# Moving the fifth product of the experts' second stage ahead of the reads of its PSUM bank, with two preparations moved

## The chip, the cores and the metric

One core of one Trainium2 chip. The time is device microseconds of one execution of the program. TensorE (PE) multiplies, VectorE (DVE), ScalarE (ACT) and GpSimd (POOL) prepare operands and read results, SyncE (SP) issues most of the transfers.

## What is computed

Linear attention with random features, then a dense mixture of four experts over its output `x` (2304 rows of 512):

```
p = domain_probs / (domain_probs.sum(-1, keepdims=True) + 1e-09)
out = np.zeros((N, D), dtype=np.float32)
for e in range(E):
    h = np.maximum(x @ w1[e], 0.0)
    out += p[:, e:e + 1] * (h @ w2[e])
```

With N = 2304, D = 512, E = 4 and 1024 hidden columns. The attention part is not touched by the change.

## The kernel before

**Visits.** The hidden columns of the four experts are cut into 8 halves of 512. One visit multiplies one half with a block of rows of `x`: its first stage is `h = relu(x @ w1)`, its second adds `p * (h @ w2)` to the accumulators `acc`. The first 11 visits are done by `plain`, the 16 that follow (row blocks of 7 tiles of 128 rows, twice 8 halves) by `fast`. Of the last 8 visits seven are "deep" (`DEEP`): in the trace they run from about 620 to 908 us. The last visit of all is not deep.

**Exact products from halves.** Each operand is split (`split`, L490 to L495) into a high part by ACT (a copy, L492) and a low part (L495, a subtraction, on POOL here), and each product is three matmuls: high by high, high by low, low by high.

**Seven products in place of eight.** `fast` computes the first stage of a visit as seven block products in each of two groups (`p1` to `p7`), whose sums are formed by ACT and DVE. A deep visit does the second stage (`sevens`, L909) in the same way: for three pairs of row tiles (`QS3`) it forms sums of `h` (`t1` in the tile `va`, `t2` in `vb`, `r11`) and uses sums of `w2` (`B`, tiles `w2s`). The operands made from sums of `h` are the pairs `T[5]`, `T[6]`, `T[7]` (tile `t_hl`). Tile 3 of the seven is computed directly (`outputs`). The second stage runs in this order on PE:

1. `X[q][:, L]`: a direct product, into the left half of the PSUM bank of `X[q]`, q = 0 to 2, amid `p7(1)`, `p3(1)` and `p4(1)` of the first stage;
2. the **fifth product**, into the right half of the same three banks, from `T[5]` (18 matmuls, L907, tiles `w2s` and `t_hl`);
3. the block product `Z` (18 matmuls), then tile 3 (12 matmuls of 512 columns, L676 to L678);
4. the sixth product, added to the left halves of `X[q]`; then a product `block(1, 1)` added to the right halves; then the seventh, and a last product from the four parts of `hs` that were overwritten.

Before the sixth product is added to the left half of `X[q]`, DVE adds what stands there to `acc` (`gather`, L693): "the reads" below. Dependencies are kept by whole PSUM tile: `X[q]` is one tile of one bank, so in this kernel an instruction that writes its right half waits for an earlier one in the program that reads its left half.

**Order of work.** Every engine does its instructions in the order in which the program issues them (`manual_schedule`); a wait holds up all that is queued behind it. Two generators, advanced by `next(...)` at fixed places, prepare the coming visit: `sides(v + 1)` the operands of the first stage (tiles `w1ah`, `w1al` from `w1r` by `direct`, split by ACT and POOL; tiles `w1sh`, `w1sl` by `fetched`, two transfers from DRAM, issued from POOL's queue), and `w2_sides(v + 1)` (`start_sides2`, `on_sides2`) those of the second (`sums_of`, four POOL additions L540 to L543 into `w2f`, then splits). After `fetched` the order in a deep visit is: `T[5]` split, then the first `sums_of` of the next visit, then all of `sevens`.

Of the kernel before, what the change touches and what calls it, by code (L numbers as in the profile page):

```python
# [9 lines left out]
ALU = mybir.AluOpType  # L10
# [4 lines left out]
def attention_moe(ctx, tc, kT, qT, kd, qd, kn, qn, vn, omT, probs, w1, w2, out):  # L15
# [10 lines left out]
    nc = tc.nc  # L26
# [42 lines left out]
    def f32(ap):  # L69
        return ap.bitcast(F32)  # L70
# [42 lines left out]
    class Pair:  # L113
# [7 lines left out]
        def load(self, which, eng=nc.sync):  # L121
            src = {"k": kT, "q": qT}[which[0]][self.b, self.hp][:, TILES[int(which[1])]]
            t = xop([P, src.shape[1]], which, F32)
            setattr(self, which, t)
            eng.dma_start(t[:D], src)
# [364 lines left out]
    def split(t, a, c, hi, lo):  # L490
        if hi is nc.scalar:
            hi.activation(a, t, AF.Copy)  # L492
        else:
            hi.tensor_copy(a, t)
        lo.tensor_tensor(c, t, f32(a), ALU.subtract)  # L495
# [95 lines left out]
    def sides(v):  # L591

        tiles = [raw.pop((v, "w1", i)) for i in range(2)]
        A, S = {}, {}

        def direct(i):
            A[i] = ah, al = pair_of(("w1ah", 3 * H), ("w1al", 3 * H))
            for r, cs in ((tiles[i][:, :2 * H], slice(0, 2 * H)), (tiles[i][:, 3 * H:], slice(2 * H, 3 * H))):
                split(r, ah[:, cs], al[:, cs], nc.scalar, nc.gpsimd)

        def add(i):
            r11, r12, r21, r22 = (tiles[i][:, j * H:(j + 1) * H] for j in range(4))
            nc.vector.tensor_tensor(r22, r21, r22, ALU.add)
            nc.vector.tensor_tensor(r21, r11, r21, ALU.subtract)
            nc.vector.tensor_tensor(r11, r22, r11, ALU.subtract)
            nc.vector.tensor_tensor(r12, r12, r11, ALU.subtract)

        def summed(i):
            S[i] = sh, sl = pair_of(("w1sh", 4 * H), ("w1sl", 4 * H))
            split(tiles[i], sh, sl, nc.scalar, nc.gpsimd)  # L610
            made[v, i] = S[i]
            parts(i)
            load("w1")

        def parts(i):
            W[v, "w1", i] = {
                p: tuple(x[:, j * H:(j + 1) * H] for x in t)
                for t, at in ((A[i], (1, 2, 4)), (S[i], (6, 3, 7, 5)))
                for j, p in enumerate(at)
            }  # L620

        def fetched(i):
            S[i] = pair_of(("w1sh", 4 * H), ("w1sl", 4 * H))
            for t, k in zip(S[i], kept[visits[v][1:3], i]):
                nc.gpsimd.dma_start(t, k)

        direct(0)
        if visits[v][0] < 2:
            yield
        else:  # L630
            load("w1")
            fetched(0)
            parts(0)
            fetched(1)
            yield
            direct(1)
            load("w1")
            parts(1)
            yield
            return  # L640
        direct(1)
        yield
        add(0)
        yield
        summed(0)
        yield
        add(1)
        yield
        summed(1)
        yield  # L650
# [31 lines left out]
    def gather(v, ps, t, cs=slice(0, DM)):  # L682
        _, e, _, c0, n = visits[v]
        i = c0 // P + t
        sc = pr[:, i, e:e + 1]
        if i not in acc:
            acc[i] = held([P, DM], "acc", F32)
        fresh = [h for h in (0, H) if cs.start <= h < cs.stop and (i, h) not in begun_at]
        begun_at.update((i, h) for h in fresh)
        if fresh:  # L690
            nc.scalar.activation(acc[i][:, cs], ps, AF.Copy, scale=sc)  # L691
        else:
            nc.vector.scalar_tensor_tensor(acc[i][:, cs], ps, sc, acc[i][:, cs], ALU.mult, ALU.add)  # L693
# [102 lines left out]
    def fast(v):  # L796
# [29 lines left out]
        def less(to, t, x, op=ALU.subtract):  # L826
            nc.vector.scalar_tensor_tensor(to, t, 0.0, x, ALU.max, op)  # L827

        def first_rows(t):
            return t[:, :WT]  # L830
# [71 lines left out]
        def seventh(q, to, a, b, start=True):  # L902
            for f in range(2):
                (xa, xc), (wa, wc) = a[f], b[f]
                xa, xc = (x[:, q * P:(q + 1) * P] for x in (xa, xc))
                for k, (x, w) in enumerate(((xa, wa), (xa, wc), (xc, wa))):
                    nc.tensor.matmul(to, x, w, start=(start and f + k == 0), stop=(f + k == 3), skip_group_check=not start)  # L907

        def sevens():  # L909

            L, R, QS3 = slice(0, H), slice(H, DM), range(3)

            def block(g, j):
                return [tuple(x[:, j * FH * P:j * FH * P + WT] for x in hs[2 * g + f]) for f in range(2)]

            def sums_of(i):
                return [tuple(x[:, f] for x in T[i]) for f in range(2)]

            def weights(g, cs):
                return [tuple(x[:, cs] for x in W[v, "w2", 2 * g + f]) for f in range(2)]  # L920

            def mixed(i, cs):
                return [tuple(x[:, cs] for x in B[f, i]) for f in range(2)]

            X, Z = [], []
            for q in QS3[:2]:
                X.append(bank("g2"))
                seventh(q, X[q][:, L], block(0, 0), weights(0, L))
            p7(1)
            less(t2[:, 1], last_rows(P_[1]["p5"]), t1[:, 1])  # L930
            X.append(bank("g2"))
            seventh(2, X[2][:, L], block(0, 0), weights(0, L))
            p3(1)
            less(t2[:, 0], last_rows(P_[1]["u2"]), t1[:, 0])
            p4(1)
            nc.gpsimd.tensor_tensor(r11, t2, r11, ALU.subtract)
            nc.scalar.activation(T[6][0], t2, AF.Copy)
            less(t1[:, 1], first_rows(P_[1]["u"]), t2[:, 1])
            for q in QS3:
                gather(v, X[q][:, L], q, L)  # L940
            nc.vector.tensor_tensor(T[6][1], t2, f32(T[6][0]), ALU.subtract)
            less(t1[:, 0], first_rows(P_[1]["p1"]), t2[:, 0])
            next(ready, None)
            split(r11, *T[7], nc.scalar, nc.gpsimd)
            for f in range(2):
                split(t1[:, f], *(x[:, FH * P:] for x in hs[f]), nc.scalar, nc.gpsimd)
            yield 1
            for q in QS3:
                seventh(q, X[q][:, R], sums_of(5), mixed(1, R), start=False)
            yield 1  # L950
            zs = []
            for q in QS3:
                if q < 2:
                    Z.append(bank("g2"))
                zs.append(Z[q // 2][:, q % 2 * H:(q % 2 + 1) * H])
                seventh(q, zs[q], block(1, 0), weights(1, L))
            for q in QS3:
                gather(v, zs[q], q, L)
            next(ready, None)
            yield 1  # L960
            ps = bank("g2")
            outputs(v, hs, ps, 3, range(FH))
            gather(v, ps, 3)
            on_sides2(v + 1)
            on_sides2(v + 1)
            yield 1
            for q in QS3:
                seventh(q, X[q][:, L], sums_of(6), mixed(0, L), start=False)
                gather(v, X[q], 4 + q)
            yield 1  # L970
            for q in QS3:
                seventh(q, X[q][:, R], block(1, 1), mixed(1, L), start=False)
                gather(v, X[q][:, R], 4 + q, L)
            on_sides2(v + 1)
            yield 1
            for q in QS3:
                seventh(q, X[q][:, L], sums_of(7), mixed(0, R), start=False)
                gather(v, X[q][:, L], 4 + q, R)
            on_sides2(v + 1)
            yield 1  # L980
            for q in QS3:
                seventh(q, X[q][:, L], [tuple(x[:, FH * P:] for x in hs[f]) for f in range(2)], weights(1, R), start=False)
                gather(v, X[q][:, L], q, R)
            for t in range(tiles):
                gathered(v, t)
            yield 1
# [24 lines left out]
        p5(1)  # L1011
        if deep:
            prepare()
        p3(0)
        p4(0)
        if deep:
            nc.scalar.activation(r11[:, 1], first_rows(P_[0]["u"]), AF.Relu)
            less(t1[:, 1], last_rows(P_[0]["p5"]), r11[:, 1])
            p6(1)
            split(t1, *T[5], nc.scalar, nc.gpsimd)  # L1020
            if v + 1 in DEEP:
                start_sides2(v + 1)
            yield from sevens()
            return
        prepare()
# [309 lines left out]
```

## Time and profile before

| | |
|---|---|
| median of 3 runs | 948.84 us (948.64 to 952.38) |
| the profiled execution | 949.2 us |
| its span in the trace | 947.4 us |
| mean granted clock of TensorE | 0.982 of full speed |
| busy, share of the span | PE 96%, DVE 61%, POOL 55%, ACT 50% |

Busy shares are averages over the whole program; the change is in seven visits of some 41 us each. In a row of the timeline the first number is the start in us from the span's start, the second the length (of all of them, where an `x18` merges 18 that follow each other), and the brackets hold the engine's idle time just before it with the instruction that ended it by the profile. A matmul's length is longer than the distance to the next, since matmuls are pipelined.

### The profile page before, as it was taken

The page shows a single profiled execution, that of the slowest core. Times are in us where ns is not written, and L with a number is a line of the kernel's source. Part 1 is how long each engine was busy: PE and PEld are TensorE (multiplying, and loading weights), DVE is VectorE, ACT ScalarE, POOL GpSimd, SP SyncE. Part 2 cuts the span into 40 slices and gives each one's busy share as a digit, 9 for nine tenths or more (in the row PEclk, how much of TensorE's full clock was granted, in tenths as well). Part 3 has the DMA queues.
Part 4 walks back from the last instruction along what each step waited for, and adds up shares of the span by engine and source line. Part 5 has one row for each costly group of instructions (what it writes and reads, how often), then busy time and mean ns, then how long its engine had stood idle before and what let it go on. Part 6 is the DMA issues. An engine that isn't in the chain of part 4 may idle for free. (4 is left out here: it accounts for less than half of the span.)

```text
span 947.4 us, 14345 instructions
## 1 busy us (share of the span) xinstructions
PE 906.0 (96%) x5286; PEld 804.1 (85%) x5286; DVE 574.4 (61%) x956; ACT 476.2 (50%) x1076; POOL 518.3 (55%) x459
## 2 busy tenths in 40 slices
PE   9999999999999999999999999998898989889898
PEld 9888888888788788888888898787897979779896
DVE  5665667776758636556765747845456565755643
ACT  6454767767645464455454453544544344353430
POOL 5655465655544533433444235668687786878630
PEclk9999999999999999999999999998998999999999
DMA  7563463553415454251434133624141432414212
GB/s 186 164 208 100 140 186 103 158 163 114 137 59 177 134 181 146 68 172 68 156 106 156 38 140 127 229 79 145 33 149 45 164 111 68 145 34 156 83 41 78
DMA packets 56583, 117.21 MB, mean 124 GB/s; under 512 B 9728, under 2 KB 18112, under 8 KB 56512
## 3 DMA queue, kind: packets, MB, share of 16 engines
q1 hardware_dynamic: 51664, 99.21, 33.0%
q0 software_dynamic: 4608, 16.78, 4.9%
q8 instruction: 42, 0.69, 0.3%
q10 hardware_dynamic: 240, 0.30, 0.1%
q14 instruction: 29, 0.24, 0.1%
HBM read 94.77 MB, written 21.50 MB: 123 GB/s over the span
## 5 line engine op out<-in xcount | busy, mean ns | idle before, releaser
L495 POOL TENSOR_TENSOR w2l<-w2r,w2h 128x512 fp32r<-128x512 f32 x93 | 122.4, 1325 | 141.3 <-ACT w2h L492 107.3
L693 DVE SCALAR_TENSOR_TENSOR acc<-g,pr,acc 128x512 f32<-128x512 f32 (+1 forms) x207 | 124.4, 618 | 89.6 <-PE g L678 57.0
L676 PE MATMUL g<-w2h,hh 128*128 128x512 f32 x368 | 147.2, 400 | 0.6 <-ACT hh L889 0.5
L678 PE MATMUL g<-w2h,hl 128*128 128x512 f32 x368 | 144.1, 392 | 0.0
L677 PE MATMUL g<-w2l,hh 128*128 128x512 f32 x368 | 143.8, 391 | 0.0
L854 DVE TENSOR_TENSOR sum<-g,sum 128x448 f32<-128x448 f32 x96 | 59.6, 621 | 97.4 <-PE g L843 96.5
L495 POOL TENSOR_TENSOR w1al<-w1r,w1ah 128x256 fp32r<-128x256 f32 (+1 forms) x77 | 87.2, 1151 | 50.1 <-ACT w1ah L492 47.1
L495 POOL TENSOR_TENSOR w1sl<-w1r,w1sh 128x512 fp32r<-128x512 f32 (+1 forms) x43 | 74.9, 1743 | 61.0 <-ACT w1sh L492 52.7
L859 ACT ACTIVATE hh<-sum 128x448 fp32r<-128x448 f32 (+1 forms) x96 | 50.9, 530 | 109.1 <-DVE sum L854 109.1
L860 DVE SCALAR_TENSOR_TENSOR hl<-sum,hh 128x448 fp32r<-128x448 f32 (+1 forms) x96 | 59.4, 618 | 73.0 <-ACT hh L859 73.0
L843 PE MATMUL g<-xbh,w1sh 128*128 128x448 f32 x256 | 94.0, 367 | 2.6 <-ACT sum L849 2.6
L843 PE MATMUL g<-xbl,w1sh 128*128 128x448 f32 x256 | 93.6, 366 | 0.0
L843 PE MATMUL g<-xbh,w1sl 128*128 128x448 f32 x256 | 93.4, 365 | 0.0
L849 ACT ACTIVATE sum<-g 128x448 f32<-128x448 f32 x96 | 51.7, 540 | 75.7 <-PE g L843 75.6
L907 PE MATMUL g<-w2s,t_hl 128*128 128x256 f32 x378 | 57.4, 314 | 28.1 <-ACT w1ah L492 24.2
L678 PEld LDWEIGHTS g<-w2h,hl 128*128 128x128 f32 x368 | 69.1, 188 | 16.1 <-DVE hl L890 0.7
L676 PEld LDWEIGHTS g<-w2h,hh 128*128 128x128 f32 x368 | 69.4, 188 | 14.6 <-ACT hh L889 0.9
L907 PEld LDWEIGHTS g<-w2s,t_hl 128*128 128x128 f32 x378 | 54.8, 219 | 31.1 <-ACT w1ah L492 26.3
L677 PEld LDWEIGHTS g<-w2l,hh 128*128 128x128 f32 x368 | 69.4, 189 | 12.2
L843 PE MATMUL g<-xbh,w1ah 128*128 128x448 f32 x192 | 70.7, 368 | 0.0
L843 PE MATMUL g<-xbh,w1al 128*128 128x448 f32 x192 | 70.2, 366 | 0.0
L843 PE MATMUL g<-xbl,w1ah 128*128 128x448 f32 x192 | 70.1, 365 | 0.0
(197 smaller groups left out, 2170.9 us busy)
## 6 DMA issues: line engine op xcount, KB each, us to landing
w1r<-in_w SPq DMA_DIRECT2D x54, 512.0 KB, 3.8
w2r<-in_w SPq DMA_DIRECT2D x108, 256.0 KB, 2.7
kept<-w1sh SPq DMA_DIRECT2D x16, 512.0 KB, 5.8
kept<-w1sl SPq DMA_DIRECT2D x16, 512.0 KB, 6.4
w1sh<-kept POOLq DMA_DIRECT2D x16, 512.0 KB, 5.9
w1sl<-kept POOLq DMA_DIRECT2D x16, 512.0 KB, 6.7
out<-acc SPq DMA_DIRECT2D x18, 256.0 KB, 2.0
va<-in_vn SPq DMA_DIRECT2D x14, 256.0 KB, 4.9
```

What stands on the lines that cost most here:

```text
L495: lo.tensor_tensor(c, t, f32(a), ALU.subtract)
L676: nc.tensor.matmul(ps, ha[:, ts_], wa, start=(c == 0), stop=False)
L677: nc.tensor.matmul(ps, ha[:, ts_], wc, start=False, stop=False)
L678: nc.tensor.matmul(ps, hc[:, ts_], wa, start=False, stop=(c == FH - 1))
L693: nc.vector.scalar_tensor_tensor(acc[i][:, cs], ps, sc, acc[i][:, cs], ALU.mult, ALU.add)
L843: nc.tensor.matmul(ps, a[:, w], x[:, k], start=(start and k + at == 0), stop=(k == 1 and at == 2), skip_group_check=not start)
L849: nc.scalar.activation(t, P_[g][where], AF.Copy)
L854: nc.vector.tensor_tensor(t, P_[g][where], t, ALU.add)
L859: nc.scalar.activation(ha, t, AF.Relu)
L860: nc.vector.scalar_tensor_tensor(hc, t, 0.0, f32(ha), ALU.max, ALU.subtract)
L907: nc.tensor.matmul(to, x, w, start=(start and f + k == 0), stop=(f + k == 3), skip_group_check=not start)
```

## The change

In deep visits: (a) the fifth product is issued before the three reads, which move behind the split of `T[7]`, the low part of `T[6]` and the last difference of `t1`; (b) the additions `sums_of` of the next visit's `w2` move from behind the split of `T[5]` to ahead of `p3(0)`; (c) the two halves of `sides` become four steps, fetch 0, direct 0, fetch 1, direct 1, at four places of the visit; the split of `T[7]` now comes ahead of both `direct` steps; (d) in the first deep visit, where accumulators are fresh, ten first writes of `acc` go from ACT to DVE. Counts of instructions per visit stay the same.

```diff
+        if visits[v][0] == 2:
+            for i in range(2):
+                fetched(i)
+                yield
+                direct(i)
+                load("w1")
+                parts(i)
+                yield
+            return
         direct(0)
-        if visits[v][0] < 2:
-            yield
-        else:
-            load("w1")
-            fetched(0)
-            parts(0)
-            fetched(1)
-            yield
-            direct(1)
-            load("w1")
-            parts(1)
-            yield
-            return
+        yield
         direct(1)
...
-        if fresh:
+        if fresh and v in DEEP:
+            nc.vector.tensor_scalar(acc[i][:, cs], ps, sc, None, ALU.mult)
+        elif fresh:
             nc.scalar.activation(acc[i][:, cs], ps, AF.Copy, scale=sc)
...
             less(t1[:, 1], first_rows(P_[1]["u"]), t2[:, 1])
+            nc.vector.tensor_tensor(T[6][1], t2, f32(T[6][0]), ALU.subtract)
+            for q in QS3:
+                seventh(q, X[q][:, R], sums_of(5), mixed(1, R), start=False)
+            split(r11, *T[7], nc.scalar, nc.gpsimd)
+            next(ready, None)
+            less(t1[:, 0], first_rows(P_[1]["p1"]), t2[:, 0])
             for q in QS3:
                 gather(v, X[q][:, L], q, L)
-            nc.vector.tensor_tensor(T[6][1], t2, f32(T[6][0]), ALU.subtract)
-            less(t1[:, 0], first_rows(P_[1]["p1"]), t2[:, 0])
             next(ready, None)
-            split(r11, *T[7], nc.scalar, nc.gpsimd)
             for f in range(2):
                 split(t1[:, f], *(x[:, FH * P:] for x in hs[f]), nc.scalar, nc.gpsimd)
-            yield 1
-            for q in QS3:
-                seventh(q, X[q][:, R], sums_of(5), mixed(1, R), start=False)
-            yield 1
+            yield 2
...
         if deep:
             prepare()
+            if v + 1 in DEEP:
+                start_sides2(v + 1)
         p3(0)
         p4(0)
...
             split(t1, *T[5], nc.scalar, nc.gpsimd)
-            if v + 1 in DEEP:
-                start_sides2(v + 1)
+            next(ready, None)
             yield from sevens()
```

PE's own order stays as it was, instruction by instruction; what it waits for differs. The fifth product of the fourth deep visit on PE before, with the engines that each row waits for (`g_7962`, `g_7969`, `g_7986` are the banks `X[0]`, `X[1]`, `X[2]`):

```order
L843 MATMUL g_7882<-xbh,w1al 128x448
L907 MATMUL g_7962<-w2s,t_hl 128x256 [waits DVE_49,Activation_49]
L907 MATMUL g_7962<-w2s,t_hl 128x256 [waits Pool_49] x2
L907 MATMUL g_7962<-w2s,t_hl 128x256 x3
L907 MATMUL g_7969<-w2s,t_hl 128x256 [waits DVE_49]
L907 MATMUL g_7969<-w2s,t_hl 128x256 x5
L907 MATMUL g_7986<-w2s,t_hl 128x256 [waits DVE_49]
```

The same place now (the three banks have the numbers 7966, 7973 and 7990):

```order
L842 MATMUL g_7882<-xbh,w1al 128x448
L906 MATMUL g_7966<-w2s,t_hl 128x256 [waits Activation_49]
L906 MATMUL g_7966<-w2s,t_hl 128x256 [waits Pool_49] x2
L906 MATMUL g_7966<-w2s,t_hl 128x256 x3
L906 MATMUL g_7973<-w2s,t_hl 128x256 x6
L906 MATMUL g_7990<-w2s,t_hl 128x256 x6
```

The three waits for DVE, one at each bank, are gone from the fifth product; those for ACT and POOL (the two halves of `T[5]`) stay. DVE at the same visit before (L693 are the reads, L941 the low part of `T[6]`, the last row the last difference of `t1`):

```order
L890 SCALAR_TENSOR_TENSOR hl<-g_7882,hh 128x448
L827 SCALAR_TENSOR_TENSOR va<-g_7882,vb 128x384
L693 SCALAR_TENSOR_TENSOR acc<-g_7962,pr,acc 128x256
L693 SCALAR_TENSOR_TENSOR acc<-g_7969,pr,acc 128x256
L693 SCALAR_TENSOR_TENSOR acc<-g_7986,pr,acc 128x256
L941 TENSOR_TENSOR t_hl<-vb,t_hl 128x768
L827 SCALAR_TENSOR_TENSOR va<-sum,vb 128x384
```

And now:

```order
L889 SCALAR_TENSOR_TENSOR hl<-g_7882,hh 128x448
L826 SCALAR_TENSOR_TENSOR va<-g_7882,vb 128x384
L938 TENSOR_TENSOR t_hl<-vb,t_hl 128x768
L826 SCALAR_TENSOR_TENSOR va<-sum,vb 128x384
L692 SCALAR_TENSOR_TENSOR acc<-g_7966,pr,acc 128x256
L692 SCALAR_TENSOR_TENSOR acc<-g_7973,pr,acc 128x256
L692 SCALAR_TENSOR_TENSOR acc<-g_7990,pr,acc 128x256
```

The reads stand behind the two operand steps. POOL at the same visit before (L540 to L543 are the sums of the next visit's `w2`, `t_hl<-va` and `t_hl<-r_7825` the low parts of `T[5]` and `T[7]`):

```order
L495 TENSOR_TENSOR w2s<-w2f,w2s 128x512 x2
L495 TENSOR_TENSOR t_hl<-va,t_hl 128x768
L540 TENSOR_TENSOR w2f<-w2r 128x256
L541 TENSOR_TENSOR w2f<-w2f,w2r 128x256
L542 TENSOR_TENSOR w2f<-w2r,w2f 128x256
L543 TENSOR_TENSOR w2f<-w2r 128x256
L936 TENSOR_TENSOR r_7825<-vb,r_7825 128x768
L495 TENSOR_TENSOR w1al<-w1r,w1ah 128x512
L495 TENSOR_TENSOR w1al<-w1r,w1ah 128x256
L625 DMA w1sh<-kept 128x1024
L625 DMA w1sl<-kept 128x1024
L625 DMA w1sh<-kept 128x1024
```

And now:

```order
L495 TENSOR_TENSOR w2s<-w2f,w2s 128x512 x2
L540 TENSOR_TENSOR w2f<-w2r 128x256
L541 TENSOR_TENSOR w2f<-w2f,w2r 128x256
L542 TENSOR_TENSOR w2f<-w2r,w2f 128x256
L543 TENSOR_TENSOR w2f<-w2r 128x256
L495 TENSOR_TENSOR t_hl<-va,t_hl 128x768
L625 DMA w1sh<-kept 128x1024
L625 DMA w1sl<-kept 128x1024
L935 TENSOR_TENSOR r_7825<-vb,r_7825 128x768
L495 TENSOR_TENSOR t_hl<-r_7825,t_hl 128x768
L495 TENSOR_TENSOR w1al<-w1r,w1ah 128x512
L495 TENSOR_TENSOR w1al<-w1r,w1ah 128x256
```

The sums stand ahead of the low part of `T[5]`, two of the four fetches ahead of `r11`, and the low part of `T[7]` ahead of the `w1al` pair.

## Rows read from the trace of the kernel before

**Rows 1.** The page's first part: busy time of each engine over the span.

```profile
PE 906.0 (96%) x5286; PEld 804.1 (85%) x5286; DVE 574.4 (61%) x956; ACT 476.2 (50%) x1076; POOL 518.3 (55%) x459
```

**Rows 2.** Waits of PE over the span: total us, times, longest us.

```profile
PE g L907 <- ACT w1ah L492: 24.2, 6, 4.2
```

**Rows 3.** Timeline of PE: `p4(1)`'s end, the fifth product, tile 3; visits 1, 4, 7.

```profile
641.58 0.37 PE L843 MATMUL g<-xbh,w1al 128*128 128x448 f32 x1
...
652.78 0.40 PE L676 MATMUL g<-w2h,hh 128*128 128x512 f32 x1
...
765.54 0.37 PE L843 MATMUL g<-xbh,w1al 128*128 128x448 f32 x1
770.14 3.51 PE L907 MATMUL g<-w2s,t_hl 128*128 128x256 f32 x18 [4.23 <-ACT w1ah L492]
...
776.01 0.40 PE L676 MATMUL g<-w2h,hh 128*128 128x512 f32 x1
...
778.76 2.31 PE L907 MATMUL g<-w2s,t_hl 128*128 128x256 f32 x18
...
785.16 0.28 PE L907 MATMUL g<-w2h,hh 128*128 128x256 f32 x1
...
888.33 0.37 PE L843 MATMUL g<-xbh,w1al 128*128 128x448 f32 x1
891.75 2.37 PE L907 MATMUL g<-w2s,t_hl 128*128 128x256 f32 x18 [3.06 <-ACT w1ah L492]
...
896.11 0.40 PE L676 MATMUL g<-w2h,hh 128*128 128x512 f32 x1
```

**Rows 4.** Stretches: length; PE, PEld, DVE, ACT, POOL busy (count); granted clock; DMA.

```profile
770.14:774.46 4.32, 4.32 (x23) 4.32 (x24) 3.45 (x4) 1.84 (x4) 4.32 (x6) 0.60 0.07 12
765.74:787.30 21.56, 17.33 (x121) 16.70 (x121) 15.20 (x26) 7.82 (x14) 19.18 (x19) 0.92 0.48 159
787.30:806.50 19.20, 19.20 (x104) 17.76 (x102) 9.01 (x15) 9.46 (x19) 11.85 (x11) 1.00 0.13 42
```

**Rows 5.** Timeline of DVE, fourth deep visit.

```profile
760.75 0.56 DVE L827 SCALAR_TENSOR_TENSOR va<-sum,r 128x384 f32<-128x384 f32 x1 [0.63 <-ACT r L1017]
...
765.24 1.09 DVE L827 SCALAR_TENSOR_TENSOR vb<-sum,va 128x384 f32<-128x384 f32 x1
...
769.52 1.26 DVE L693 SCALAR_TENSOR_TENSOR acc<-g,pr,acc 128x256 f32<-128x256 f32 x3
...
778.96 3.34 DVE L693 SCALAR_TENSOR_TENSOR acc<-g,pr,acc 128x512 f32<-128x512 f32 x5 [2.20 <-PE g L678]
```

**Rows 6.** Timeline of ACT (first row) and POOL, fourth deep visit.

```profile
761.35 0.85 ACT L492 ACTIVATE t_hl<-va 128x768 fp32r<-128x768 f32 x1 [0.26 <-DVE va L827]
...
757.51 1.30 POOL L495 TENSOR_TENSOR w2s<-w2f,w2s 128x512 fp32r<-128x512 f32 x1 [0.22 <-ACT w2s L492]
762.27 1.88 POOL L495 TENSOR_TENSOR t_hl<-va,t_hl 128x768 fp32r<-128x768 f32 x1 [3.46 <-ACT t_hl L492]
764.10 0.74 POOL L540 TENSOR_TENSOR w2f<-w2r 128x256 f32<-128x256 f32 x1
...
766.88 0.72 POOL L543 TENSOR_TENSOR w2f<-w2r 128x256 f32<-128x256 f32 x1
...
770.47 2.71 POOL L495 TENSOR_TENSOR w1al<-w1r,w1ah 128x512 fp32r<-128x512 f32 x2
...
777.09 2.00 POOL L495 TENSOR_TENSOR hl<-va,hh 128x384 fp32r<-128x384 f32 x2
```

**Rows 7.** Timeline of DVE, then POOL, last deep visit.

```profile
891.13 1.26 DVE L693 SCALAR_TENSOR_TENSOR acc<-g,pr,acc 128x256 f32<-128x256 f32 x3
892.31 1.90 DVE L941 TENSOR_TENSOR t_hl<-vb,t_hl 128x768 fp32r<-128x768 f32 x1
894.13 1.09 DVE L827 SCALAR_TENSOR_TENSOR va<-sum,vb 128x384 f32<-128x384 f32 x1
...
890.29 1.84 POOL L936 TENSOR_TENSOR r<-vb,r 128x768 f32<-128x768 f32 x1 [3.37 <-DVE vb L827]
```

## The prediction

> **What bounds the kernel now.** I read the busy shares first: PE is busy for 906.0 of 947.4 us, and no other engine for more than 61% [rows 1]. So time can come only from PE's idle 41 us, from PE's work at a low clock, or from PE work taken away, and this change takes none away. Next, PE's waits. One kind holds most of the idle time: six waits of up to 4.2 us, 24.2 us together, all ahead of L907 [rows 2]. The timeline shows the place, the fifth product of each deep visit: in the fourth, PE issues the last matmul of `p4(1)` at 765.54 and the first of the fifth product at 770.14 [rows 3].
>
> What ends that wait? The profile names a split of `w1ah` on ACT, which the fifth product does not read. The order of instructions tells more: at each of its three banks the product waits for DVE, and the reads of these banks begin at 769.52 [rows 5], 0.62 us before the product does. Its own operand was done long before: the low half of `T[5]` ended at 762.27 + 1.88 = 764.15 [rows 6]. I take the reads as what ends last. They are late because DVE has the differences and low parts of `p3(1)` and `p4(1)` to do first.
>
> The wait costs twice. In the 4.32 us after it the granted clock is 0.60 [rows 4], a mixture of the half level (1.2 GHz) and the full one (2.4 GHz). The 36 matmuls of the fifth product and of `Z` then take 776.01 - 770.14 = 5.87 us in the fourth visit. In the last deep visit, where the wait was 3.06 us, they take 896.11 - 891.75 = 4.36 us [rows 3], 0.12 us each.
>
> **The change, part by part.**
>
> *The fifth product ahead of the reads.* From the last matmul of `p4(1)` to the first of tile 3 a visit without wait needs 4.36 us plus one matmul of 448 columns. Twelve matmuls of 512 columns take 778.76 - 776.01 = 2.75 us [rows 3], so this one is 2.75 / 12 x 448 / 512 = 0.20, together 4.56 us. The trace has 652.78 - 641.58 = 11.20 in the first deep visit, 10.47 in the fourth, 7.78 in the seventh [rows 3]: losses of 6.64, 5.91 and 3.22 us. With the fourth for the five in the middle the sum is 6.64 + 5 x 5.91 + 3.22 = 39.4 us. All of it lies on PE, which never waits otherwise in these stretches, so all of it shortens the span if nothing else is late.
>
> What is late next? Below, times are from PE's arrival at the fifth product (+0; 765.74 in the fourth visit, 888.53 in the seventh).
>
> *`T[5]` and the sums of `w2` (part b).* On POOL the four additions, 764.10 to 767.60, 3.50 us, now go ahead of the low half of `T[5]`. They can start when the `w2s` split ends, 757.51 + 1.30 = 758.81, so they end at 762.31, in what was an idle gap of 3.46 us [rows 6]. The high half on ACT ended at 762.20 [rows 6]. It waits for a DVE difference of 0.56 us (760.75), which will now run beside the additions; the like one that ran beside them before took 1.09 [rows 5]. So I add 0.53: high half at 762.73, low half from there for 1.88 to 764.61. PE's third matmul is the first to read it, at 765.74 + 2 x 0.12 = 765.98. Spare: 1.37 us. No wait.
>
> *The reads behind two DVE operations (part a).* The seventh visit has no additions on POOL at this place and serves as the model. There the reads began at 891.13, +2.60 [rows 7]. At this point the low part of `T[6]` now starts; the next difference follows 894.13 - 892.31 = 1.82 us later and takes 1.09 [rows 7], so the reads begin at +5.51 and end 1.26 later, +6.77. PE wants the first at the sixth product, at +4.36 + 2.75 = +7.11, the others later: no wait. Behind them stand the three reads of `Z` (1.26, to +8.03), tile 3 and `X[0]`. Five reads took 3.34 us, four of them of 512 columns [rows 5]; less 1.26 / 3 for the short one that is 0.73 each, so `X[0]` is read at +9.49. PE wants to add `block(1, 1)` to that bank after the sixth product, whose length is (785.16 - 778.76) / 3 = 2.13 us [rows 3], at +9.24. I charge 0.25 us per visit, 1.8 us in seven. DVE had idled 2.20 us ahead of these reads [rows 5]; this was the cover.
>
> *The order of `T[7]`, `direct` and the fetches (part c).* The operand that PE needs last is the pair of overwritten `hs` parts, at +7.11 + 6.40 + 0.25 = +13.76. On POOL `r11` ends at 890.29 + 1.84, +3.60 [rows 7]. From the `w1al` split at 770.47 to these parts at 777.09 POOL had 6.62 us of work [rows 6]: the `w1al` pair, four fetches and the low half of `T[7]`. Now two of the four fetches come earlier, and the high half of `T[7]` on ACT, 0.85 by the like split [rows 6], stands ahead. The parts start by +3.60 + 0.85 + 6.62 = +11.07 and take 2.00: done at +13.07, 0.7 us to spare. The first `w1al` pair is needed only by the next visit's `p1`, after +15. Cost 0; if POOL ran 0.7 us later, the excess would go to the end one to one.
>
> *First writes on DVE (part d).* Ten in the first deep visit. The other six visits have their additions at these places on DVE already, so the walk above covers them. Cost 0, at most the same 0.25.
>
> **Sum.** 949.2 us for the profiled execution (947.4 span and 1.8 around it), less 39.4, plus 1.8: 911.6. That execution lies 0.4 above the median of 948.84; I forecast 911.5. Its own bounds: if the unshown middle visits lose as much as the first, 5 x 0.73 = 3.7 more and no new wait, about 906; with 0.7 us of new wait a visit, some 915.
>
> **The rivals.**
>
> *POOL becomes the bound.* POOL is busy for 19.18 + 11.85 = 31.03 of a visit of 40.76 us [rows 4]; the visit is to shrink to some 35. The additions took 3.50 us where four of the shortest, 0.72, take 2.88: beside DVE work POOL stretches by a fifth. If all of POOL's work stretched by a tenth, 3.1 us, the low half of `T[5]` would be late by 3.1 - 1.37 = 1.7 us in each visit that has additions ahead of it, six of them: 10 us, about 922. Against it: the stretch was local. Here the Trainium skill is harsher than the rows: "SBUF — State Buffer", "Who interferes with whom", says that a DVE instruction with two SBUF inputs and a GpSimd instruction that reads SBUF exclude each other, the second waiting for the whole first. By it each of the two DVE differences ahead of `T[5]` could be held for a whole addition, 0.88 us, and the low half would end at 764.15 + 1.75 = 765.90, with 0.1 us to spare; the sum stays, the margin goes. The rows so far show 0.53 per instruction. Chance 0.12.
>
> *DVE's reads come late.* If T[6]'s low part and the reads slip by another 1 us, PE waits at `block(1, 1)` by as much: seven visits, 7 us, about 918.5. For it: my margin there is already negative. Against it: the slow values, 1.90 and 1.09, are in the walk. Chance 0.14.
>
> *The wait stays.* If ACT, which the profile names, really ended it, the product would still start at +4.4, and the time stays at 949. Against it: ACT must deliver only the high half of `T[5]`, done 3.5 us earlier. Chance 0.03.
>
> *Slower.* The reads now queue behind the fifth product and two more DVE operations; PE could wait at the sixth product instead and lose the clock there. To end above 954 the seven visits must lose 39.4 + 4.7 = 44 us at the new place, 6.3 each: about 4.8 of wait and 1.5 of clock. The reads would have to be done at +11.9 instead of about +6. No instruction in that part of DVE's queue is longer than 1.90 us. Chance 0.02.
>
> **How the numbers follow.** The forecast gets 0.69. Its range of 906 to 915, the late reads at 918.5 and POOL's 922 are taken in: 907 to 922 leaves out about 0.13, made of the wait that stays, the slower case, half of POOL's case and the lowest corner. A measurement of this kernel tells about 0.5%, 4.7 us, from no change. All cases but two are faster by much more: faster 0.95, same 0.03, slower 0.02.
>
> **What would show it.** After: no idle time ahead of the fifth product in any deep visit, granted clock 1.00 in the 9 us that follow, deep visits 35 us apart, the low half of `T[5]` done over 1 us ahead of PE, the reads from about +5.5, and a few tenths of wait at `block(1, 1)`. I am wrong if PE waits for POOL at `T[5]` or the `hs` parts, or if a wait of over 3 us appears at the sixth product with the clock down behind it.

## The result, and the profile after

The changed kernel takes 911.85 us (median of 4 runs, 911.01 to 912.63), the kernel before beside it 948.74 (4 runs): ratio 0.9612, 95% interval 0.9571 to 0.9654. In a later comparison on one chip, with six runs, it took 911.97 at 0.9618 (0.9592 to 0.9643). The forecast was 911.5 us.

First the page of the changed kernel: span, busy times, and the row of the granted clock in 40 slices.

```profile
span 909.4 us, 14363 instructions
## 1 busy us (share of the span) xinstructions
PE 893.9 (98%) x5286; PEld 793.2 (87%) x5286; DVE 580.7 (64%) x966; ACT 470.4 (52%) x1066; POOL 516.2 (57%) x459
...
PEclk9999999999999999999999999999999999999999
```

PE's idle time fell from 41 to 15.5 us, and PE itself is busy for 12 us less [rows 1] with the same 5286 matmuls: that is work that no longer runs at the low clock. The waits of PE, longest first:

```profile
PE g L842 <- ACT sum L848: 3.1, 2, 1.6
PE g L906 <- ACT hh L888: 1.8, 1, 1.8
...
PE g L906 <- DVE hl L889: 0.9, 2, 0.7
```

The six waits at the fifth product [rows 2] are gone, and so is a seventh, in the first deep visit. The wait of 1.8 us for `hh` stands ahead of `X[0]` in the first deep visit, where the kernel before had it too. The timeline of PE in the fourth deep visit (start, length, operation):

```profile
742.65 0.28 PE L906 MATMUL g<-w2l,hh 128*128 128x256 f32 x1
743.04 0.39 PE L906 MATMUL g<-w2h,hl 128*128 128x256 f32 x1
...
748.27 0.36 PE L842 MATMUL g<-xbh,w1al 128*128 128x448 f32 x1
748.47 2.29 PE L906 MATMUL g<-w2s,t_hl 128*128 128x256 f32 x18
...
752.75 0.40 PE L673 MATMUL g<-w2h,hh 128*128 128x512 f32 x1
...
755.50 2.31 PE L906 MATMUL g<-w2s,t_hl 128*128 128x256 f32 x18
757.65 0.40 PE L906 MATMUL g<-w2s,hh 128*128 128x256 f32 x2
```

The fifth product starts 0.20 us after the last matmul of `p4(1)`, and tile 3 4.48 us after it, where it took 10.47 [rows 3]. Over the seven visits this distance was 11.20, 10.46, 10.97, 10.47, 10.46, 11.02 and 7.78, together 72.36 us; it is now 5.77, 4.48, 4.49 and four times 4.48, together 32.66. So 39.7 us went here. The span fell by 38.0; in the rest of the first six visits 2.0 us came back, and the first deep visit reached its fifth product 0.4 earlier.

Three stretches of the same visit (length; PE, PEld, DVE, ACT, POOL busy; granted clock; DMA), fifth product and `Z`, whole second stage, first stage of the next visit:

```profile
748.47:752.79 4.32, 4.32 (x38) 4.32 (x37) 3.67 (x6) 2.20 (x4) 1.87 (x1) 1.00 0.70 240
748.47:764.06 15.59, 15.59 (x122) 15.10 (x121) 13.36 (x25) 7.50 (x14) 12.55 (x12) 1.00 0.53 178
764.06:783.28 19.22, 19.15 (x103) 17.66 (x101) 10.46 (x15) 9.57 (x19) 18.00 (x18) 1.00 0.22 76
```

In this execution the clock is at its full level throughout these stretches where it was 0.60 behind the wait [rows 4], and PE has no gap in the second stage. POOL is now busy for 12.55 + 18.00 = 30.6 of 34.8 us. What DVE did around this place:

```profile
740.60 1.17 DVE L826 SCALAR_TENSOR_TENSOR va<-sum,r 128x384 f32<-128x384 f32 x1
741.70 0.76 DVE L859 SCALAR_TENSOR_TENSOR hl<-sum,hh 128x64 fp32r<-128x64 f32 x1
742.38 0.61 DVE L889 SCALAR_TENSOR_TENSOR hl<-g,hh 128x448 fp32r<-128x448 f32 x1
743.62 0.80 DVE L826 SCALAR_TENSOR_TENSOR va<-sum,r 128x384 f32<-128x384 f32 x1 [0.63 <-ACT r L1018]
...
746.79 0.92 DVE L859 SCALAR_TENSOR_TENSOR hl<-sum,hh 128x448 fp32r<-128x448 f32 x1 [0.65 <-ACT hh L858]
...
750.91 0.55 DVE L826 SCALAR_TENSOR_TENSOR va<-g,vb 128x384 f32<-128x384 f32 x1
751.37 1.86 DVE L938 TENSOR_TENSOR t_hl<-vb,t_hl 128x768 fp32r<-128x768 f32 x1
753.15 0.55 DVE L826 SCALAR_TENSOR_TENSOR va<-sum,vb 128x384 f32<-128x384 f32 x1
753.62 3.75 DVE L692 SCALAR_TENSOR_TENSOR acc<-g,pr,acc 128x256 f32<-128x256 f32 x8
```

And POOL beside it:

```profile
740.05 1.31 POOL L495 TENSOR_TENSOR w2s<-w2f,w2s 128x512 fp32r<-128x512 f32 x1 [0.31 <-ACT w2s L492]
741.44 0.93 POOL L540 TENSOR_TENSOR w2f<-w2r 128x256 f32<-128x256 f32 x1
...
743.96 1.06 POOL L543 TENSOR_TENSOR w2f<-w2r 128x256 f32<-128x256 f32 x1
745.37 1.86 POOL L495 TENSOR_TENSOR t_hl<-va,t_hl 128x768 fp32r<-128x768 f32 x1 [0.35 <-ACT t_hl L492]
747.18 0.57 POOL L625 DMA_DIRECT2D w1sh<-kept  x1
...
750.54 1.87 POOL L935 TENSOR_TENSOR r<-vb,r 128x768 f32<-128x768 f32 x1 [2.26 <-DVE vb L826]
753.38 2.04 POOL L495 TENSOR_TENSOR t_hl<-r,t_hl 128x768 fp32r<-128x768 f32 x1 [0.96 <-ACT t_hl L492]
```

The reads begin at 753.62, 5.15 us behind PE's arrival at 748.47, and nobody waits for them. The low half of `T[5]` ends at 747.23, 1.24 us ahead of PE. And the matmul at 743.04 stands 0.39 us behind its neighbour: here is what came back. It is the first to read the low part that DVE made at 742.38, behind two DVE instructions that take 1.17 and 0.76 us beside POOL's splits and sums. That place, `X[0]`, loses some 0.45 us in each of the second to the sixth visit.

### The profile page after: what moved, and what is told of

It is laid out like the page before. It is cut to its first block, busy times and chain, and to the rows that moved or that the text cites. A ratio compares the mean times of both kernels' runs of the same rounds, so it can differ in the third digit from the quotient of the medians.

```text
span 909.4 us, 14363 instructions
## 1 busy us (share of the span) xinstructions
PE 893.9 (98%) x5286; PEld 793.2 (87%) x5286; DVE 580.7 (64%) x966; ACT 470.4 (52%) x1066; POOL 516.2 (57%) x459
## 4 chain that ended last, share of the span: by engine, by line
PE 83%; DVE 8%; DMA 2%; ACT 2%; POOL 2%; issue 2%; SPq 1%; DVEq 0%; POOLq 0%; ACTq 0%
PE g L842 24%; PE g L906 11%; PE g L673 9%; PE g L675 9%; PE g L674 9%; PE g L658 3%; PE g L660 3%; PE g L659 3%; PE kv L314 2%; PE k_ps L266 1%; PE q_ps L266 1%; PE qt_ps L325 1%; PE k_ps L148 1%; DMA w2r<-in_w 1%; DVE hl L859 1%
## 5 line engine op out<-in xcount | busy, mean ns | idle before, releaser
L692 DVE SCALAR_TENSOR_TENSOR acc<-g,pr,acc 128x512 f32<-128x512 f32 (+1 forms) x207 | 122.2, 615 | 54.4 <-PE g L675 42.2
L859 DVE SCALAR_TENSOR_TENSOR hl<-sum,hh 128x448 fp32r<-128x448 f32 (+1 forms) x96 | 67.8, 706 | 73.9 <-ACT hh L858 73.9
L495 POOL TENSOR_TENSOR w1al<-w1r,w1ah 128x256 fp32r<-128x256 f32 (+1 forms) x77 | 82.3, 1086 | 52.4 <-ACT w1ah L492 49.2
L492 ACT ACTIVATE w2h<-w2r 128x512 fp32r<-128x512 f32 x90 | 55.1, 626 | 18.0 <-DMA w2r<-in_w 12.8
L842 PEld LDWEIGHTS g<-xbh,w1sh 128*128 128x128 f32 x256 | 48.1, 188 | 8.7 <-ACT sum L848 3.9
```

The costliest lines, as they stand in the source:

```text
L842: nc.tensor.matmul(ps, a[:, w], x[:, k], start=(start and k + at == 0), stop=(k == 1 and at == 2), skip_group_check=not start)
L859: nc.vector.scalar_tensor_tensor(hc, t, 0.0, f32(ha), ALU.max, ALU.subtract)
```

## The experiments

Times are medians beside the kernel before on the same chip (948.1 to 949.0 us), with the ratio's 95% interval.

**1. Part (a) alone.** Of the change only the order of the reads:

```diff
-            for q in QS3:
-                gather(v, X[q][:, L], q, L)
             nc.vector.tensor_tensor(T[6][1], t2, f32(T[6][0]), ALU.subtract)
+            for q in QS3:
+                seventh(q, X[q][:, R], sums_of(5), mixed(1, R), start=False)
             less(t1[:, 0], first_rows(P_[1]["p1"]), t2[:, 0])
+            for q in QS3:
+                gather(v, X[q][:, L], q, L)
...
-            yield 1
-            for q in QS3:
-                seventh(q, X[q][:, R], sums_of(5), mixed(1, R), start=False)
-            yield 1
+            yield 2
```

> Part (a) alone on the kernel before: the fifth product ahead of the reads; sums of w2, T[7], direct steps and fetches where they were. Theory (the reads ended the wait, and the low clock behind it is the second half of its price): nearly the whole gain, 913 to 917 us; the fifth product starts 0.2 us after p4(1), a wait of about 0.6 us goes to Z (DVE slowed by the sums on POOL) and up to 0.3 to the seventh product (T[7]'s low half behind four fetches). Rival (it needs the moves on POOL too: sums ahead, T[7] ahead): a wait of over 2 us per visit at the seventh product or the hs parts, above 925 us.

Measured 920.55 us, ratio 0.9698 (0.9675 to 0.9722): between the two. The waits of PE in the fourth visit:

```profile
755.95 0.39 PE L907 MATMUL g<-w2h,hl 128*128 128x256 f32 x1 [0.58 <-DVE hl L890]
...
763.41 0.50 PE L907 MATMUL g<-w2s,hh 128*128 128x256 f32 x2 [0.76 <-DVE acc L693]
```

The fifth product waits for nothing in any visit, so part (a) takes the long wait away by itself, and with it 28 of the 37 us. The wait at `Z` is there as expected (tile 3 at 5.32 instead of 4.48 us). The second one is at `block(1, 1)`, for a read on DVE, not at the seventh product for POOL: neither side had that. It is even there in the last visit, which has no sums on POOL.

**2. Part (b) alone.** `start_sides2(v + 1)` ahead of `p3(0)`, all else as before:

```diff
             prepare()
+            if v + 1 in DEEP:
+                start_sides2(v + 1)
         p3(0)
...
             split(t1, *T[5], nc.scalar, nc.gpsimd)
-            if v + 1 in DEEP:
-                start_sides2(v + 1)
```

> Part (b) alone on the kernel before: the next visit's sums of w2 ahead of T[5]'s low half on POOL; the fifth product still waits for the reads. Theory (wait and clock are separate prices): DVE, without additions beside it, reaches the reads as in the last deep visit, the wait falls from 4.4 to 3.2 us and the clock stays up, so each of six visits loses 3.2 instead of 5.9 to 6.7: 17 us less, and 2.6 back for contention at X[0], 932 to 938 us. Rival 1 (the clock falls behind any such wait): 6 x 1.2, about 942. Rival 2 (the sums' place costs nothing): 949.

Measured 948.35 us, ratio 0.9992 (0.9966 to 1.0018): no gain, the figure of rival 2 but not for its reason, and my theory fell twice over. The wait shortened less than expected: the fifth product starts 3.74 us behind `p4(1)`'s last matmul where it was 4.60, 0.3 more than in the last visit, since `T[5]`'s low part now runs on POOL beside a DVE low part and holds it up. And the clock mostly fell all the same. The fifth product of the third and of the last visit in this run:

```profile
726.28 2.37 PE L907 MATMUL g<-w2s,t_hl 128*128 128x256 f32 x18 [3.37 <-ACT w1ah L492]
...
885.57 4.18 PE L907 MATMUL g<-w2s,t_hl 128*128 128x256 f32 x18 [3.06 <-ACT w1ah L492]
```

and the stretches behind it in the third, the fourth and the last (the clock is the seventh number):

```profile
726.28:730.50 4.22, 4.22 (x35) 4.22 (x36) 3.86 (x5) 1.73 (x4) 4.22 (x6) 1.00 0.14 17
764.85:769.00 4.15, 4.15 (x22) 4.15 (x23) 3.45 (x4) 1.68 (x4) 4.15 (x6) 0.59 0.09 8
885.57:891.00 5.43, 5.43 (x25) 5.43 (x26) 3.46 (x4) 2.78 (x6) 5.43 (x8) 0.50 0.22 63
```

A wait of 3.37 us is followed by the full clock in the third visit and by 0.59 in the fourth; the wait of 3.06 us in the last visit, which cost no clock in the kernel before [rows 3], is followed here by 0.50. The length of the wait does not decide it. Nor did the shorter wait bring nothing in every run: the ten runs lie between 943.40 us, with a mean granted clock of 0.989, and 952.62, with 0.974. In these runs a lower clock goes with a longer time; that it took away what the shorter wait gave is likely, not shown.

**3. Part (c) alone.** `sides` in four steps, as in the change, and `T[7]`'s split ahead of both `direct` steps, the reads where they were:

```diff
             for q in QS3:
                 gather(v, X[q][:, L], q, L)
             nc.vector.tensor_tensor(T[6][1], t2, f32(T[6][0]), ALU.subtract)
+            split(r11, *T[7], nc.scalar, nc.gpsimd)
+            next(ready, None)
             less(t1[:, 0], first_rows(P_[1]["p1"]), t2[:, 0])
             next(ready, None)
-            split(r11, *T[7], nc.scalar, nc.gpsimd)
...
                 start_sides2(v + 1)
+            next(ready, None)
             yield from sevens()
```

> Part (c) alone on the kernel before: fetch and direct in four steps, the split of T[7] ahead of both direct steps; reads and sums where they were. Theory (the reads on DVE end the wait): the fifth product starts no earlier, 947 to 951 us. Rival (the wait is for the split of w1ah on ACT, which the profile names): that split now stands behind T[7], the profile names another releaser and the time changes by more than 5 us.

Measured 949.71 us, ratio 1.0006 (0.9978 to 1.0034). The split of `w1ah` now stands behind `T[7]`, and the profile names another releaser of the same wait:

```profile
769.36 2.96 PE L904 MATMUL g<-w2s,t_hl 128*128 128x256 f32 x13 [4.23 <-DVE acc L690]
```

Again 4.23 us, now put down to the reads; of the rival only the other name came, not its change of over 5 us. That the split of `w1ah` did not end the wait is shown.

**4. The change without part (b).** On the changed kernel, `start_sides2(v + 1)` back behind `T[5]`'s split:

```diff
             prepare()
-            if v + 1 in DEEP:
-                start_sides2(v + 1)
         p3(0)
...
             split(t1, *T[5], nc.scalar, nc.gpsimd)
+            if v + 1 in DEEP:
+                start_sides2(v + 1)
             next(ready, None)
```

> The changed kernel with part (b) undone: the sums of w2 behind T[5]'s low half again. Theory: the sums' place matters little once the reads are out of the way; the 0.4 us wait at X[0] in six visits goes, one of about 0.7 us at Z comes (DVE's low parts beside the additions), 912 to 916 us. Rival (POOL is the bound, and the idle gap ahead of T[5] has to be used): r11, T[7] and the hs parts late on POOL, over 1.5 us per visit, above 921.

Measured 916.01 us, ratio 0.9656 (0.9636 to 0.9677), at the upper edge of what was expected. A visit takes about 36.2 us instead of 35.2. The gap at `X[0]` is gone; at `Z` 0.8 to 0.9 us are lost, and at `block(1, 1)` 0.4 to 0.5. So the sums have a better place ahead of `T[5]`, by 4 us over the kernel; POOL is no bound at either place.

**5. The wait filled with matmuls.** On the kernel before, ahead of the fifth product:

```diff
+            pad = bank("g1")
+            for _ in range(12):
+                nc.tensor.matmul(pad, hs[0][0][:, :P], W[v, "w2", 0][0], start=True, stop=True)
             for q in QS3:
                 seventh(q, X[q][:, R], sums_of(5), mixed(1, R), start=False)
```

> The kernel before with twelve matmuls of 512 columns, whose result nobody reads, put on PE just ahead of the fifth product: 2.75 us of added work in a wait of 4.4. Theory (the low clock behind the wait is a price of its own): the fifth product starts when it did, PE is idle for only 1.7 us, the clock stays at the full level, and the 36 matmuls take 4.4 instead of 5.9 to 6.9 us: about 11 us less over seven visits although there is more work, 936 to 940 us. Rival (the loss behind the wait is something else, such as DVE or POOL still late): 947 to 950, tile 3 as late as before.

Measured 940.30 us, ratio 0.9925 (0.9902 to 0.9949), 0.3 us above the range of the theory and far from the rival's. PE in the fourth visit, and two stretches: up to the fifth product, and behind it:

```profile
764.94 2.88 PE L950 MATMUL g<-w2h,hh 128*128 128x512 f32 x12
769.34 2.36 PE L907 MATMUL g<-w2s,t_hl 128*128 128x256 f32 x18 [1.52 <-ACT w1ah L492]
...
773.70 0.40 PE L676 MATMUL g<-w2h,hh 128*128 128x512 f32 x1
```

```profile
764.74:769.34 4.60, 3.08 (x14) 2.28 (x13) 3.95 (x8) 2.52 (x5) 3.46 (x4) 1.00 0.00 0
769.34:773.70 4.36, 4.36 (x37) 4.36 (x38) 4.00 (x6) 1.87 (x5) 4.36 (x6) 1.00 0.09 19
```

The fifth product starts as late as before (4.60 us), and the 36 matmuls then take 4.36 us in place of 5.87: the kernel is faster with 84 matmuls more. From the first to the last deep visit it needs 235.7 us where the kernel before needed 246.8, 11.0 less; the whole time fell by 7.8 in the median. The profiled run, the longest of the four at 943.31, fell by 5.9 against that of the kernel before, since it came 5.1 us later to the first deep visit, which the edit does not touch and which I leave unexplained (the kernel before spread from 945 to 950 us beside it). So some 11 of the 39.7 us at this place were low clock, and nearly 29 were waiting.

**6. First writes on ACT.** The changed kernel with part (d) undone:

```diff
-        if fresh and v in DEEP:
-            nc.vector.tensor_scalar(acc[i][:, cs], ps, sc, None, ALU.mult)
-        elif fresh:
+        if fresh:
             nc.scalar.activation(acc[i][:, cs], ps, AF.Copy, scale=sc)
```

> The changed kernel with part (d) undone: in the first deep visit the ten first writes of the accumulators on ACT again. Theory (one visit, where neither engine bounds): within 2 us of the changed kernel, 910 to 914. Rival (ACT's writes hold T[7]'s high half or the splits behind them, so PE waits at the sixth or seventh product of that visit): 2 to 5 us more, 914 to 917.

Measured 912.78 us, ratio 0.9631 (0.9614 to 0.9649). The first deep visit takes 36.49 us, with (d) 36.54, but the two lose their time at different places. Without (d) PE waits in that visit at `block(1, 1)`, for one of ACT's first writes:

```profile
654.02 0.50 PE L904 MATMUL g<-w2s,hh 128*128 128x256 f32 x2 [1.30 <-ACT acc L688]
```

This is the rival's mechanism, at another product. With (d) this wait is in neither trace of the changed kernel: in one the visit loses 1.3 us ahead of tile 3 instead, in the other (experiment 10), where the clock fell ahead of the fifth product as it did here, it takes 34.94 us. The medians, 912.78 here against 911.85 and 911.97, differ by 0.8 to 0.9 us. Part (d) may be worth that; it is inside the spread.

**7. The first difference of `t1` behind `p4(0)`'s low part.** On the changed kernel:

```diff
-                if f == 0:
-                    less(t1[:, 0], last_rows(t), r11[:, 0])
...
         if deep:
+            less(t1[:, 0], last_rows(P_[0]["u2"]), r11[:, 0])
             nc.scalar.activation(r11[:, 1], first_rows(P_[0]["u"]), AF.Relu)
```

> The changed kernel with the first difference of t1 issued behind p4(0)'s low part on DVE instead of ahead of it. Theory (the 0.4 us that each of six visits loses at X[0] comes from this DVE instruction, held by a POOL instruction beside it): that wait goes, T[5] stays in time, 2 to 3 us less, 908.5 to 910.5. Rival (the wait is set by ACT's part or by the 64-column low part alone): no change, 911 to 913; or T[5] comes late and a wait appears at the fifth product.

Measured 911.33 us, ratio 0.9617 (0.9599 to 0.9634). The gap at `X[0]` is gone in every visit from the second on, which shows where it came from, and the six periods between the first and the last fifth product add up to 2.0 us less in the trace. But 1.65 of these 2.0 are the first period, 34.89 us in place of 36.54, and the changed kernel itself took 34.94 there in its other trace (experiment 10). In three of the visits without the gap PE comes late at the first matmul of `p7(1)` instead, by 0.22 to 0.50 us, for ACT. In the median 0.5 us is gained, inside the spread: 911.33 lies in the range of the rival (no change), not in that of the theory, though the gap was where the theory put it.

**8. Also a reordered first visit.** The last two splits of `w2` sums of that visit behind `p4(0)`, the next visit's sums behind `T[5]`. Beside the edit of number 7:

```diff
-            steps2 = [2, 1, 1, 1, 1, 1, 1, 1] if v == DEEP[0] else [1, 1, 1, 0, 0, 1, 1, 0]
+            steps2 = [2, 1, 1, 1, 1, 1, 0, 0] if v == DEEP[0] else [1, 1, 1, 0, 0, 1, 1, 0]
...
-            if v + 1 in DEEP:
+            if v > DEEP[0] and v + 1 in DEEP:
                 start_sides2(v + 1)
...
+            if v == DEEP[0]:
+                for _ in range(3):
+                    next(ready2, None)
             less(t1[:, 1], last_rows(P_[0]["p5"]), r11[:, 1])
             p6(1)
             split(t1, *T[5], nc.scalar, nc.gpsimd)
+            if v == DEEP[0]:
+                start_sides2(v + 1)
```

> As the run with the late difference, and in the first deep visit the last two splits of the w2 sums are issued behind p4(0) and the next visit's sums behind T[5]'s split. Theory (ACT stands in that visit at a split that waits for POOL, with p4(0)'s high part queued behind it): the 2 us wait at X[0] in the first visit and part of the 1.3 us at Z go, 2 to 3 us less than the run with the late difference alone, 906 to 908.5. Rival (POOL is late in that visit anyway): the wait moves to the fifth product, no gain.

Measured 910.37 us, ratio 0.9603 (0.9582 to 0.9623). This is above the range of the theory. The wait of 1.8 us for ACT in the first visit is gone; one of 0.64 us for ACT stands at `p7(1)` instead, the fifth product comes 1.0 us earlier than in the changed kernel, and the wait for DVE at `Z` is 1.12 us where it was 0.73. Most of it came back elsewhere, as the rival had it, though at other places.

**9. Parts (a) and (b).** Without (c) and (d): the edits of numbers 1 and 2 together on the kernel before.

> Parts (a) and (b) on the kernel before, without (c) and (d): the split of T[7] behind the w1al pair on POOL, all four fetches together. Theory (with the w1al split on POOL beside it, the last difference of t1 on DVE takes 1.1 to 1.6 us instead of 0.55, the reads end later and X[0] is read late): no wait at Z, a wait of 0.5 to 0.8 us at block(1, 1) in each of seven visits, none at the seventh product, 915 to 918 us. Rival ((c) mattered only for what POOL delivers, T[7] and the hs parts): a wait at the seventh product or behind it and none at block(1, 1); or no wait, 911 to 913.

Measured 917.18 us, ratio 0.9663 (0.9639 to 0.9687), as the theory had it. The wait on PE, the last difference on DVE and the split beside it on POOL, fourth visit:

```profile
761.58 0.50 PE L907 MATMUL g<-w2s,hh 128*128 128x256 f32 x2 [0.75 <-DVE acc L693]
...
756.21 1.65 DVE L827 SCALAR_TENSOR_TENSOR va<-sum,vb 128x384 f32<-128x384 f32 x1
...
755.43 3.03 POOL L495 TENSOR_TENSOR w1al<-w1r,w1ah 128x512 fp32r<-128x512 f32 x2
```

The difference takes 1.65 us here and 0.55 in the changed kernel, where POOL stands idle when it begins (at 753.15), waiting for `T[7]`'s high half until 753.38. That is what (c) is worth: not what POOL delivers, but what it leaves DVE. No wait is at `Z` or at the seventh product.

**10 and 11. The changed kernel and number 8 once more, on one chip.**

> The changed kernel itself, beside the next run on one chip: 911 to 913 us.

> The kernel with the late difference and the reordered first visit once more, beside the changed kernel: 1 to 2 us less than that, if the two waits that it removes in the trace are worth what their rows say; 0 if they come back elsewhere.

Measured 911.97 us, ratio 0.9618 (0.9592 to 0.9643), and 909.20, ratio 0.9581 (0.9556 to 0.9606). The second gain, 2.8 us, is more than was expected. The intervals of the ratios overlap, but each of the five runs of number 8's kernel (908.58 to 911.10) is shorter than each of the six of the changed kernel (911.27 to 917.13): a little better, by about 0.3%, on this chip.

The trace of number 10 is a second trace of the changed kernel. In the first deep visit the same wait ahead of `X[0]` ends at 635.33 in the first trace and at 636.44 in this one. PE there, and the stretch from it to the fifth product, in the first trace:

```profile
635.33 0.39 PE L906 MATMUL g<-w2h,hh 128*128 128x256 f32 x1 [1.83 <-ACT hh L888]
635.33:641.42 6.09, 5.93 (x33) 5.39 (x34) 3.98 (x4) 2.36 (x4) 5.86 (x6) 1.00 0.08 31
```

and in this one:

```profile
636.44 0.39 PE L906 MATMUL g<-w2h,hh 128*128 128x256 f32 x1 [1.81 <-ACT hh L888]
636.44:644.11 7.67, 7.51 (x34) 6.75 (x34) 4.58 (x6) 2.35 (x4) 6.98 (x8) 0.78 0.14 44
```

One and the same kernel keeps the clock behind this wait once and loses it once, at a cost of 1.58 us. Behind the lower clock PE then finds the operands of `Z` ready: from `p4(1)`'s last matmul to tile 3 it needs 4.49 us, not 5.77. Number 8 takes the 1.8 us wait away, and in both of its traces the clock stays up here; that this is where its gain comes from is not shown.

Put together: (b) and (c) alone give nothing, since the fifth product waits on. Behind (a), which gives 28 us, (b) gives 3.4 (experiments 1 and 9) and (c) with (d) 5.3 more (9 and the changed kernel).

## Why the prediction was right, and where it was not

- *What ends the wait.* Right: the reads. Experiment 3 moved the ACT instruction that the profile named, and the wait stayed, with the reads named; experiment 1 moved the reads, and the wait went.
- *The price.* The sum of 39.4 us came to 39.7. The third and sixth visits lost 0.5 us more than the fourth, which stood for them; the stretch without a wait took 4.48, not 4.56, 0.6 in seven visits; and in the first visit 1.3 us of its loss stayed in this trace, none in that of experiment 10. These three nearly cancel, so that the sum came so close is in part luck. That the price has two parts is shown by experiment 5.
- *The clock behind a shorter wait.* The prediction used the last visit as the case with a 3.06 us wait and no clock lost. As a fact of that visit it was right; my expectation for experiment 2, that waits of this length keep the clock, was not, and in experiment 10 even a wait of 1.81 us did not.
- *`T[5]` and the sums.* The low half ended 1.48 us ahead of PE's third matmul, where 1.37 was forecast. POOL did not become the bound; it had gaps of 0.35 and 2.26 us in the rows above.
- *The reads.* They began at +5.15, not +5.51. The term that was mis-sized is the last difference, "takes 1.09": a row with the `w1al` split beside it, when part (c) takes that split away. Measured 0.55. So the charge of 0.25 us at `block(1, 1)` came to nothing; with the old order of `T[7]` it is 0.75 in the trace (experiment 9).
- *The residual.* I put 1.8 us in at `block(1, 1)`; 2.0 came, at `X[0]`, a place that I did not walk. I had looked at what the sums do to `T[5]` behind them, not at the low part of `p4(0)`, ahead of `T[5]` in DVE's queue, which PE needs earlier. The sum was right there partly by luck.
- *Parts (c) and (d).* The cost of 0 for (d) holds. For (c) it was too little: I priced it by what PE waits for from POOL, and it was worth some 5 us through DVE, with (d) in the same comparison.
- *DVE beside POOL.* I took +0.53 us from a row and set the rule of the Trainium skill beside it as the harsher case. The rows after agree with that rule; the last section has them.

## What to carry to other kernels

A wait of the busiest engine costs its length and may cost some 40 per cent of it again in clock behind it (11 on 29 us here); look at the matmuls after the wait before pricing it, and do not count on a shorter wait to keep the clock. When an engine in order waits for readers of a bank, moving its write ahead of them pays in full only if everything behind the readers still comes in time (alone it gave 28 of 37 us here), so walk the reader's queue with the neighbours that it will have, not with those of the old row. The instruction that a profile names as a wait's end can be a bystander that ended at about the same time: check whether the waiting instruction reads it.

## What the hardware showed that I had not expected

**A DVE instruction with two SBUF operands stood still until POOL's instruction ended.** The clearest place is the first deep visit of the changed kernel, DVE and POOL:

```profile
639.75 2.25 DVE L859 SCALAR_TENSOR_TENSOR hl<-sum,hh 128x448 fp32r<-128x448 f32 x1 [0.65 <-ACT hh L858]
...
639.65 1.86 POOL L495 TENSOR_TENSOR t_hl<-va,t_hl 128x768 fp32r<-128x768 f32 x1
```

DVE began 0.10 us behind POOL, and ended at 642.00, 0.49 after POOL's end at 641.51. In the fourth visit DVE began much later in POOL's instruction (at 746.79, 1.42 behind POOL at 745.37), and ended at 747.71, 0.48 after POOL's end at 747.23. One took 2.25 us, the other 0.92, and both end half a microsecond after POOL. The same form takes 0.62 to 0.63 us where POOL is idle. Nor are the two alone: thirteen differences `va<-sum,r` of the changed kernel began within an instruction of POOL; they took 0.79 to 1.35 us, and each ended 0.41 to 0.42 us after POOL's. That agrees with the rule of the Trainium skill, "SBUF — State Buffer", "Who interferes with whom": a DVE instruction with two inputs in SBUF and a GpSimd instruction that reads SBUF exclude each other, and the second waits for all of the first. A DVE instruction with one of its two operands in PSUM was not held: the difference at 750.91 began 0.37 us behind POOL's instruction of 750.54, took 0.55 us and ended 0.95 ahead of it.

**The same wait, with and without a fall of the clock.** 3.06 us ahead of the fifth product of the last visit: full clock behind it in the kernel before, 0.50 in experiment 2. And 1.8 us ahead of `X[0]` in the first visit: full clock in one trace of the changed kernel, 0.78 up to the fifth product in the other. What decides it these runs do not show.
